# First loads, first 1/std, first transpositions and the v ring of a linear-attention and feed-forward kernel

## The chip, the cores and the metric

The kernel runs on one core of a Trainium2 chip. The metric is the device time of one execution in microseconds (us), lower is better. Every kernel is executed several times, beside the kernel before on the same chip, and one execution is profiled. "Faster" and "slower" are used for differences above 2%.

Engines in the profile: PE is TensorE (matrix products), PEld its weight loads, DVE is VectorE, ACT is ScalarE, POOL is GpSimd, SP is the engine that issues most transfers.

## The reference, cut to what matters

```python
x = A_x                                            # 2048 x 640, bf16
h  = x + A(layernorm(x), wqkv, w_phi, wo)          # 32 heads of 20, two softmax feature maps (+ and -)
h2 = h + B(layernorm(h), w_gate, w_up, w_down)     # (gelu(x Wg) * (x Wu)) Wd, 1536 wide
# in A: pk = k @ w_phi per head; phi_k = [softmax(pk), softmax(-pk)]; kv = phi_k^T v; q likewise; o = phi_q kv / den
```

The kernel cuts the 2048 rows into 16 tiles of 128 rows. It folds w_phi into the q and k weights (products `wa`, evicted to `Wk` and `Wq`), so that k and q tiles come out of one product each.

## The kernel before: the parts that the change and the argument touch

LayerNorm of one tile: statistics on VectorE, 1/std as a power on GpSimd, then the normalised tile on VectorE (`ln`), five 128x128 transpositions on TensorE (`tp`) and a copy to `LN1T`. From tile 6 on, the transposition is done by a DMA.

```python
def ln_stats(pool, tiles, tag, act=True, between=None):
    ...
    ve = small(pool, [P, n], "ve" + tag)
    nc.gpsimd.tensor_scalar_add(ve, mv[:, :, 1], EPS)
    rstd = small(pool, [P, n], "rstd" + tag)
    nc.gpsimd.tensor_tensor(rstd, ve, nhalf[:, 0:n], op=ALU.pow)
```

The first loads come from two issuing engines, and the head of the program is:

```python
nc.sync.dma_start(x_sb[0][:, 0:1, :], x_v[:, 0:1, :])        # tile 0
nc.scalar.dma_start(x_sb[0][:, 1:2, :], x_v[:, 1:2, :])      # tile 1
... # tiles 2-3, Wv, wphi, tiles 4-7, WkT (a DMA transposition)
warm(NWARM)                      # 10 products of zeros, 512 wide
...
ln_st(0, act=False)
ln_st(1, act=False)
ln_ap(0, on_pe=True)
ln_tp(0)
warm(WA)
ln_st(2, act=False, between=lambda: ln_ap(1, on_pe=True))
ln_tp(1)
warm(WB)
ln_st(3, act=False)
ln_ap(2, on_pe=True)
... # BD, the block-diagonal form of w_phi, on VectorE
ln_ap(3, on_pe=True)
v_part(0, 0, 1, 2, 3, 4)
v_part(1, 0, 1)
ln_tp(2)
v_part(1, 2, 3, 4)
ln_tp(3)
v_ev(0)                          # ScalarE evicts v tiles from PSUM to vS
v_ev(1)
v_tile(2)
... # tiles 4 to 7, fold of Wk: evictions in turn by ScalarE (d even) and VectorE (d odd)
```

Then a loop over the 16 tiles: a k tile, its exponentials (`E`), the v tile four ahead, normalisation six ahead, sums and products for the k side (`sk`, `rs`, `vt`), two kv tiles at a time. `vS` is a ring of six v tiles; at tile `T3 = 3` the PSUM pool is exchanged for one with a buffer less, which makes room for `kvp`. The attention of the later tiles is woven into the feed-forward stage:

```python
weave(gus(0, 256, 512) + downs(0, (2, 3)), attn_at(7, 1, SHORT2))   # tile 7 starts at unit 1
```

The softmax here doesn't subtract the row's maximum and nothing guards it: scores larger than these inputs give would overflow.

## Time and profile before

| | before |
|---|---|
| time, median | 281.47 us (280.92 to 281.91, 3 runs); later, beside the changed kernel, 281.43 |
| span of the profiled execution | 279.4 us |
| TensorE busy | 97% |
| first transposition | 6.60 us |
| ScalarE's copy of tile 3's transposition starts | 12.17 us |
| transposition after the first k tile starts | 18.26 us |
| first q product | 62.36 us |
| first 512-wide gate product | 144.07 us |
| last product | 276.15 us |

The timeline from 12 to 19 us, ScalarE and the k tile (start, duration, engine, line, operation, out<-in; the bracket is the idle time before it and what ended it):

```profile
12.17 0.69 ACT L139 COPY LN1T<-tp 128x640 bf16<-128x640 bf16 x1 [1.00 <-PE tp L138]
12.76 1.89 ACT L271 CAST vS<-pv 128x640 bf16<-128x640 f32 x3
14.52 0.72 ACT L224 CAST Wk<-wa 128x640 bf16<-128x640 f32 x1
...
16.11 1.29 ACT L224 CAST Wk<-wa 128x640 bf16<-128x640 f32 x2
16.86 1.57 PE L251 MATMUL pk<-Wk,LN1T 128*128 128x320 bf16 x10 [0.15 <-ACT Wk L224]
```

The copy of the fourth transposition opens a row of eight ScalarE items (itself, three v evictions, a Wk copy, a v eviction, two Wk copies); the k tile begins when the second of its three Wk copies is done. The list of transfers (last number: microseconds from issue to landing), tiles 1 and 0 of x:

```profile
x_sb<-in_A_x_dram ACTq DMA_DIRECT2D x1, 160.0 KB, 3.3
x_sb<-in_A_x_dram SPq DMA_DIRECT2D x1, 160.0 KB, 3.1
```

### The profile page before, as it was taken

Reading aid. Unit: us, or ns where it says so; the run is one execution under the profiler, and the core shown is the slowest. Engines: PE = TensorE matmul, PEld = TensorE weight load, DVE = VectorE, ACT = ScalarE, POOL = GpSimd, SP = SyncE. Lnnn points to the kernel's source line nnn. Section 1 sums busy time; section 2 is a strip of 40 time slices with the busy share of each in tenths; the row PEclk is TensorE's granted clock in tenths of the full one; section 3 lists DMA queues with packets and bytes.
Section 4 is the critical chain, followed back from the end, with each engine's and each line's share of the span. In section 5 each row is a group of like instructions: output and inputs, shape, how many; then the busy total and the mean of one; then the engine's idle time right before and its main releaser. Section 6 shows DMA issues by size and latency. Waiting matters only on the chain.

```text
span 279.4 us, 5750 instructions
## 1 busy us (share of the span) xinstructions
PE 271.9 (97%) x2326; PEld 171.5 (61%) x2326; DVE 166.0 (59%) x289; ACT 139.9 (50%) x226; POOL 96.5 (35%) x211
## 2 busy tenths in 40 slices
PE   5899999999999999999999999999999999999995
PEld 2676677774655788788764555675455567444573
DVE  5899998789396586676324848322667532333222
ACT  2589888758596847355434454413446340222200
POOL 5448986794302216453401243300135230000000
PEclk9999999999999999999999999999999999999999
DMA  7991323694440021322520103221031513000011
GB/s 231 265 260 25 55 49 46 176 396 158 142 145 0 2 45 29 70 50 68 52 70 2 36 20 66 42 77 47 2 47 23 74 23 94 26 1 0 0 49 47
DMA packets 40347, 21.05 MB, mean 75 GB/s; under 512 B 33152, under 2 KB 38400, under 8 KB 40320
## 3 DMA queue, kind: packets, MB, share of 16 engines
q1 hardware_dynamic: 39376, 20.16, 28.8%
q10 hardware_dynamic: 944, 0.52, 0.7%
q8 instruction: 18, 0.29, 0.5%
q14 instruction: 9, 0.07, 0.1%
HBM read 10.18 MB, written 2.62 MB: 46 GB/s over the span
## 4 chain that ended last, share of the span: by engine, by line
PE 89%; DVE 4%; ACT 3%; DMA 1%; POOL 1%; issue 1%; ACTq 0%
PE gu L554 37%; PE pd L569 19%; PE pq L338 8%; PE po L509 8%; PE pk L251 7%; PE pv L251 5%; PE ab L449 2%; PE kvp L316 2%; DVE stats L106 1%; DMA x_sb<-in_A_x_dram 1%; DVE sk L290 1%; ACT E L283 1%; POOL rstd L114 1%; ACT Eq L343 1%; PE wa L215 1%
## 5 line engine op out<-in xcount | busy, mean ns | idle before, releaser
L557 ACT ACTIVATE g<-gu 128x512 bf16<-128x512 f32 (+1 forms) x60 | 30.7, 512 | 76.1 <-PE gu L554 75.1
L560 DVE TENSOR_TENSOR GT<-gu,g 128x512 bf16<-128x512 f32 (+1 forms) x60 | 34.5, 581 | 53.6 <-ACT g L557 53.4
L554 PE MATMUL gu<-LN2T,Wg 128*128 128x512 bf16 (+1 forms) x300 | 61.9, 337 | 0.5 <-DVE GT L560 0.4
L554 PE MATMUL gu<-LN2T,Wu 128*128 128x512 bf16 (+1 forms) x300 | 61.7, 336 | 0.0
L569 PE MATMUL pd<-Wd,GT 128*128 128x320 bf16 x384 | 53.8, 299 | 0.0
L569 PEld LDWEIGHTS <-GT 128*128 128x128 bf16 x384 | 37.4, 98 | 15.7 <-DVE GT L560 0.9
L554 PEld LDWEIGHTS <-Wu 128*128 128x128 bf16 x300 | 29.4, 98 | 22.6
L554 PEld LDWEIGHTS <-Wg 128*128 128x128 bf16 x300 | 28.4, 98 | 21.3 <-issue 0.5
L251 PEld LDWEIGHTS <-LN1T 128*128 128x128 bf16 x300 | 28.5, 98 | 11.6 <-issue 0.7
L298 POOL TENSOR_TENSOR vt<-vS,rs 128x672 bf16<-128x672 bf16 x22 | 29.2, 1345 | 9.1 <-DVE rs L294 8.5
L575 DVE TENSOR_TENSOR y<-pd,x_sb 128x640 bf16<-128x640 f32 (+1 forms) x17 | 13.3, 784 | 30.6 <-PE pd L569 30.6
L457 ACT COPY AB<-ab 128x704 f32<-128x704 f32 x28 | 19.5, 748 | 13.7 <-PE ab L449 13.5
L290 DVE TENSOR_REDUCE sk<-E 128x64 f32<-128x1280 bf16 x16 | 23.3, 1455 | 3.4 <-ACT E L283 3.4
L490 DVE TENSOR_TENSOR tt<-AB,w 128x1280 bf16<-128x1280 f32 x16 | 23.8, 1486 | 2.1 <-POOL w L483 2.0
L251 PE MATMUL pk<-Wk,LN1T 128*128 128x320 bf16 x160 | 24.1, 299 | 0.4 <-ACT E L283 0.3
L509 PE MATMUL po<-Wo,oT 128*128 128x320 bf16 x160 | 24.4, 299 | 0.0
L283 ACT ACTIVATE E<-pk 128x640 bf16<-128x640 f32 x32 | 20.8, 705 | 6.9 <-PE pk L251 6.7
L338 PE MATMUL pq<-LN1T,Wq 128*128 128x512 bf16 x100 | 22.9, 379 | 0.0
L251 PE MATMUL pv<-Wv,LN1T 128*128 128x320 bf16 x140 | 21.3, 299 | 0.0
L343 ACT ACTIVATE Eq<-pq 128x1024 bf16<-128x1024 f32 (+1 forms) x22 | 19.4, 950 | 3.7 <-PE pq L338 3.7
L509 PEld LDWEIGHTS <-oT 128*128 128x128 bf16 x160 | 15.6, 98 | 7.2 <-ACT oT L139 0.2
L125 ACT ACTIVATE ln<-x_sb,v,rstd 128x640 bf16<-128x640 bf16 x14 | 12.9, 919 | 10.5 <-POOL v L537 10.3
(80 smaller groups left out, 258.8 us busy)
## 6 DMA issues: line engine op xcount, KB each, us to landing
out_dram<-y SPq DMA_DIRECT2D x15, 160.0 KB, 1.8
Wg<-in_B_w_gate_dram SPq DMA_DIRECT2D x1, 1920.0 KB, 7.6
Wu<-in_B_w_up_dram SPq DMA_DIRECT2D x1, 1920.0 KB, 15.1
Wd<-in_B_w_down_dram SPq DMA_DIRECT2D x1, 1920.0 KB, 8.0
x_sb<-in_A_x_dram SPq DMA_DIRECT2D x2, 640.0 KB, 4.7
Wo<-in_A_wo_dram SPq DMA_DIRECT2D x1, 800.0 KB, 9.3
x_sb<-in_A_x_dram SPq DMA_DIRECT2D x2, 320.0 KB, 4.8
Wv<-in_A_wqkv_dram SPq DMA_DIRECT2D x2, 320.0 KB, 6.2
```

The lines of the kernel that those rows point to most:

```text
L251: nc.tensor.matmul(ps[:, u, 0:HD], lhsT=lnT(t, c), rhs=W[:, c, u * HD:(u + 1) * HD], start=(c == 0), stop=(c == NC - 1))
L283: nc.scalar.activation(Ek[t][:, s, :].rearrange("p (u f) -> p u f", u=2), pk[:, :, 0:HD], ACTF.Exp, scale=(1.0 if s == 0 else -1.0))
L290: nc.vector.reduce_sum(sk, Ek[t].rearrange("p s (h f) -> p (s h) f", f=Dh), axis=AX.X)
L298: eng.tensor_tensor(vt[:, s], vS[t % 6], rs[:, s * H:(s + 1) * H, None].to_broadcast([P, H, VC]), ALU.mult)
L338: nc.tensor.matmul(pqs[j][:, i, :], lhsT=Wq2[:, kc, c * P:(c + 1) * P], rhs=LN1T[b][:, kc, :], start=(kc == 0), stop=(kc == NC - 1))
L343: nc.scalar.activation(Eq[j][:, :, s, :], pqs[j][:, 0:len(QG[j])], ACTF.Exp, scale=(1.0, -1.0)[s])
L490: nc.vector.tensor_tensor(tt.rearrange("p s (h f) -> p s h f", f=Dh), num, w[:, :, :, None].to_broadcast([P, 2, H, Dh]), ALU.mult)
L509: nc.tensor.matmul(po[:, u, 0:HD], lhsT=st[t][:, c, :], rhs=Wo[:, c, u * HD:(u + 1) * HD], start=(c == 0), stop=(c == NC - 1))
L554: nc.tensor.matmul(gu[:, i, 0:n], lhsT=W[:, c, f * P:(f + 1) * P], rhs=LN2T[b][:, c, a0:a1], start=(c == 0), stop=(c == NC - 1))
L557: nc.scalar.activation(g[:, 0:n], gu[:, 0, 0:n], ACTF.Gelu_apprx_tanh)
L560: nc.vector.tensor_tensor(st[b, "g", f][:, a0:a1], gu[:, 1, 0:n], g[:, 0:n], ALU.mult)
L569: nc.tensor.matmul(pd[:, u, 0:HD], lhsT=st[b, "g", f][:, tl * P:(tl + 1) * P], rhs=Wd[:, f, u * HD:(u + 1) * HD], start=(f == 0), stop=(f ...
```

## The change

The intent, as far as the code tells: bring tile 0 in sooner, shorten the way from its statistics to its normalised form, give TensorE v products as early as they can run, take the ring of v tiles out of VectorE's way, and shorten the last store.

```diff
-    NWARM = 10
+    NWARM = 11
+    KA, QA = (0,1,2,4), (0,1,2,3,4)      # which folds ScalarE evicts (was: even ones)
-    WA, WB = 2,0
-    T3 = 3
+    WA = 1
+    T3 = 4
... ln_stats, for tiles 0, 1 and 2 (log=True)
+            nc.scalar.activation(ve, mv[:, :, 1], ACTF.Ln, bias=eps)
+            nc.scalar.activation(rstd, ve, ACTF.Exp, scale=-0.5)
... ring
-    vS = [... for i in range(6)]
+    vS = [... for i in range(8)]
... loads: all on nc.sync, in the order tile 0, tile 1, Wv 0-3, tiles 2-3, Wv 4, wphi, tiles 4-5, WkT, tiles 6-7
... head
+    ln_st(0, act=False, log=True)
+    ln_st(1, act=False, between=lambda: ln_ap(0, on_pe=True), log=True)
+    ln_tp(0, True)                       # VectorE copies it
     warm(WA)
+    ln_ap(1, on_pe=True)
+    v_part(0, 0, 1)
+    ln_tp(1)
+    ln_st(2, act=False, log=True)
+    v_part(0, 2, 3, 4)
+    v_part(1, 0, 1, 2)
+    ln_st(3, act=False, between=lambda: ln_ap(2, on_pe=True))
+    ln_tp(2)
+    ln_ap(3, on_pe=True)
     ... BD ...
+    v_part(1, 3, 4)
+    v_part(2, 0, 1, 2)
+    ln_tp(3)
+    v_part(2, 3, 4)
     v_ev(0)
     v_ev(1)
+    v_ev(2)
... last tile
+        cuts = [(0, 192), (192, HD)] if last and u == 1 else [(0, HD)]
... weave
-    attn_at(7, 1, SHORT2)
+    attn_at(7, 3, SHORT2)
```

More of the change, by code (lines that the diff above doesn't have):

```diff
@@ L86 @@
     nhalf = const.tile([P, 2], F32, name="nhalf")
+    eps = const.tile([P, 1], F32, name="eps")
     def eq(t, c, s):
@@ L97, in gtile, with ln_stats @@
         return psG.tile([P, 2, 512], F32, name=name, tag="G")
-    def ln_stats(pool, tiles, tag, act=True, between=None):
+    def ln_stats(pool, tiles, tag, act=True, between=None, log=False):
         n = len(tiles)
@@ L111, in ln_stats @@
         ve = small(pool, [P, n], "ve" + tag)
-        nc.gpsimd.tensor_scalar_add(ve, mv[:, :, 1], EPS)
         rstd = small(pool, [P, n], "rstd" + tag)
-        nc.gpsimd.tensor_tensor(rstd, ve, nhalf[:, 0:n], op=ALU.pow)
+        if log:
+            nc.scalar.activation(ve, mv[:, :, 1], ACTF.Ln, bias=eps)
+            nc.scalar.activation(rstd, ve, ACTF.Exp, scale=-0.5)
+        else:
+            nc.gpsimd.tensor_scalar_add(ve, mv[:, :, 1], EPS)
+            nc.gpsimd.tensor_tensor(rstd, ve, nhalf[:, 0:n], op=ALU.pow)
         mr = small(pool, [P, n], "mr" + tag)
@@ L151 @@
     acc = p1.tile([P, NC, 4, VC], F32, name="acc")
-    vS = [p1.tile([P, H, VC], BF16, name=f"vS{i}") for i in range(6)]
+    vS = [p1.tile([P, H, VC], BF16, name=f"vS{i}") for i in range(8)]
     fp_cm = tc.tile_pool(name="fp", bufs=1, side="right", reuse_waits="tile")
@@ L160 @@
     nc.gpsimd.memset(nhalf, -0.5)
+    nc.gpsimd.memset(eps, EPS)
     nc.sync.dma_start(x_sb[0][:, 0:1, :], x_v[:, 0:1, :])
-    nc.scalar.dma_start(x_sb[0][:, 1:2, :], x_v[:, 1:2, :])
+    nc.sync.dma_start(x_sb[0][:, 1:2, :], x_v[:, 1:2, :])
+    nc.scalar.add_instruction(mybir.InstLoadActFuncSet(name=nc.get_next_instruction_name(), act_func_set_id=6))
+    nc.sync.dma_start(Wv[:, 0:2, :], w_v[:, 0:2, 2 * D:3 * D])
+    nc.sync.dma_start(Wv[:, 2:4, :], w_v[:, 2:4, 2 * D:3 * D])
     nc.sync.dma_start(x_sb[0][:, 2:4, :], x_v[:, 2:4, :])
-    for c0, c1 in ((0, 2), (2, 4), (4, 5)):
-        nc.sync.dma_start(Wv[:, c0:c1, :], w_v[:, c0:c1, 2 * D:3 * D])
-    ones = fp.tile([P, 2], F32, name="ones")
-    nc.scalar.activation(ones, nhalf, ACTF.Exp)
-    nc.scalar.dma_start(wphi, phi_v.rearrange("(c p) f -> p c f", p=P))
+    nc.sync.dma_start(Wv[:, 4:5, :], w_v[:, 4:5, 2 * D:3 * D])
+    nc.sync.dma_start(wphi, phi_v.rearrange("(c p) f -> p c f", p=P))
     nc.sync.dma_start(x_sb[1][:, 0:2, :], x_v[:, 4:6, :])
-    nc.scalar.dma_start(x_sb[1][:, 2:4, :], x_v[:, 6:8, :])
     nc.sync.dma_start_transpose(WkT, A_wqkv[:, D:2 * D])
+    nc.sync.dma_start(x_sb[1][:, 2:4, :], x_v[:, 6:8, :])
     wo_v = A_wo.rearrange("(c p) n -> p c n", p=P)
@@ L182 @@
     nc.vector.memset(zero, 0.0)
-    for i in range(6):
+    for i in range(8):
         nc.vector.memset(vS[i][:, :, Dh], 1.0)
@@ L222, in fold @@
                 src = src.rearrange("p u (c f) -> p u c f", c=NC)
-            if d % 2 == 0:
+            if d in (QA if halves else KA):
                 nc.scalar.copy(dst, src)
@@ L228, with ln_st @@
     lnp, Ek, Vt = {}, {}, {}
-    def ln_st(*tiles, act=True, between=None):
-        for t, v in zip(tiles, ln_stats(p1, [x_sb[t // 4][:, t % 4, :] for t in tiles], "1", act, between)):
+    def ln_st(*tiles, act=True, between=None, log=False):
+        for t, v in zip(tiles, ln_stats(p1, [x_sb[t // 4][:, t % 4, :] for t in tiles], "1", act, between, log)):
             lnp[t] = v
@@ L270, in v_ev @@
     def v_ev(t):
-        nc.scalar.copy(vS[t % 6][:, :, 0:Dh].rearrange("p (u h) f -> p u h f", u=2),
+        nc.scalar.copy(vS[t % 8][:, :, 0:Dh].rearrange("p (u h) f -> p u h f", u=2),
                        pv[t][:, :, 0:HD].rearrange("p u (h f) -> p u h f", f=Dh))
@@ L297, in mult @@
         def mult(s, eng):
-            eng.tensor_tensor(vt[:, s], vS[t % 6], rs[:, s * H:(s + 1) * H, None].to_broadcast([P, H, VC]), ALU.mult)
+            eng.tensor_tensor(vt[:, s], vS[t % 8], rs[:, s * H:(s + 1) * H, None].to_broadcast([P, H, VC]), ALU.mult)
         mult(1, nc.gpsimd)
@@ L343, in q_exp @@
             nc.scalar.activation(Eq[j][:, :, s, :], pqs[j][:, 0:len(QG[j])], ACTF.Exp, scale=(1.0, -1.0)[s])
-    ln_st(0, act=False)
-    ln_st(1, act=False)
-    ln_ap(0, on_pe=True)
-    ln_tp(0)
+    ln_st(0, act=False, log=True)
+    ln_st(1, act=False, between=lambda: ln_ap(0, on_pe=True), log=True)
+    ln_tp(0, True)
     warm(WA)
-    ln_st(2, act=False, between=lambda: ln_ap(1, on_pe=True))
+    ln_ap(1, on_pe=True)
+    v_part(0, 0, 1)
     ln_tp(1)
-    warm(WB)
-    ln_st(3, act=False)
-    ln_ap(2, on_pe=True)
+    ln_st(2, act=False, log=True)
[4 more added lines that the diff above has]
+    ln_ap(3, on_pe=True)
     nc.vector.tensor_tensor(BD, wphi[:, :, None, :].to_broadcast([P, NC, 8, Dh]),
                             hmask[:, :, :, None].to_broadcast([P, NC, 8, Dh]), ALU.mult)
-    ln_ap(3, on_pe=True)
-    v_part(0, 0, 1, 2, 3, 4)
-    v_part(1, 0, 1)
-    ln_tp(2)
-    v_part(1, 2, 3, 4)
+    v_part(1, 3, 4)
+    v_part(2, 0, 1, 2)
     ln_tp(3)
+    v_part(2, 3, 4)
     v_ev(0)
     v_ev(1)
-    v_tile(2)
+    v_ev(2)
     ln_st(4, 5, act=False)
@@ L567, in down @@
             pd = gtile("pd")
-        for f in range(NF):
-            nc.tensor.matmul(pd[:, u, 0:HD], lhsT=st[b, "g", f][:, tl * P:(tl + 1) * P],
-                             rhs=Wd[:, f, u * HD:(u + 1) * HD],
-                             start=(f == 0), stop=(f == NF - 1))
         last = b == NB - 1 and tl == 3
-        if u == 1 or last:
-            a = u if last else 0
-            nc.vector.tensor_tensor(y.rearrange("p (u f) -> p u f", u=2)[:, a:u + 1], pd[:, a:u + 1, 0:HD],
-                                    x_sb[b][:, tl, :].rearrange("p (u f) -> p u f", u=2)[:, a:u + 1], ALU.add)
-            stores.append((lag, o_v[:, 4 * b + tl, a * HD:(u + 1) * HD], y[:, a * HD:(u + 1) * HD]))
-            if b == NB - 1 and tl >= 2:
-                store(lag)
+        cuts = [(0, 192), (192, HD)] if last and u == 1 else [(0, HD)]
+        for n0, n1 in cuts:
+            if n0:
+                pd = gtile("pd")
+            for f in range(NF):
+                nc.tensor.matmul(pd[:, u, n0:n1], lhsT=st[b, "g", f][:, tl * P:(tl + 1) * P],
+                                 rhs=Wd[:, f, u * HD + n0:u * HD + n1], start=(f == 0), stop=(f == NF - 1))
+            if u == 1 or last:
+                a = u if last else 0
+                r = lambda x: x.rearrange("p (u f) -> p u f", u=2)[:, a:u + 1, n0:n1]
+                nc.vector.tensor_tensor(r(y), pd[:, a:u + 1, n0:n1], r(x_sb[b][:, tl, :]), ALU.add)
+                f0, f1 = a * HD + n0, u * HD + n1
+                stores.append((lag, o_v[:, 4 * b + tl, f0:f1], y[:, f0:f1]))
+                if b == NB - 1 and tl >= 2:
+                    store(lag)
     later, stores, lag = [], [], 3
@@ L658 @@
           attn_at(6, 13, SHORT2))
-    weave(gus(0, 256, 512) + downs(0, (2, 3)), attn_at(7, 1, SHORT2))
+    weave(gus(0, 256, 512) + downs(0, (2, 3)), attn_at(7, 3, SHORT2))
     for b in range(1, NB):
```

## The prediction

> **What bounds the kernel now.** I read the page first: the busy shares, the slices and the shares of the chain.
>
> ```profile
> PE 271.9 (97%) x2326; PEld 171.5 (61%) x2326; DVE 166.0 (59%) x289; ACT 139.9 (50%) x226; POOL 96.5 (35%) x211
> ...
> PE   5899999999999999999999999999999999999995
> ...
> PE 89%; DVE 4%; ACT 3%; DMA 1%; POOL 1%; issue 1%; ACTq 0%
> ```
>
> TensorE sets the time. Its slices are full except for the first two or three and the last, so only the head, the tail and single waits between can be won. The chain of waits in order of time says when TensorE begins to lead (start, duration, what):
>
> ```profile
> 0.79 3.14 DMA x_sb<-in_A_x_dram
> 3.96 0.90 DVE stats L106 x2
> 4.88 0.21 DVE mv L110
> ...
> 6.67 0.57 POOL rstd L114
> 7.26 0.45 DVE ln L130
> ...
> 9.74 1.42 POOL rstd L114
> 11.18 0.46 DVE ln L130
> 11.63 0.05 issue
> 11.68 0.45 PE tp L138 x5
> 12.13 2.04 PE pv L251 x15
> ...
> 16.21 0.60 ACT Wk L224
> 16.81 0.04 issue
> 16.86 1.57 PE pk L251 x10
> 18.43 0.28 PE tp L138 x5
> ```
>
> Until 11.68 the chain is load, statistics, 1/std and normalised tile, on VectorE and GpSimd. From about 18.4 TensorE's own work leads. From the first transposition at 6.60 to the transposition that follows the first k tile (18.26 in the timeline) TensorE has 5 transpositions of 0.28, 2 warm-up products of 0.22, 40 v products and 10 k products of 0.136 (1.36 for ten) and 5 folds of 0.32: 1.40 + 0.43 + 5.44 + 1.36 + 1.60 = 10.2 us in 11.7, so about 1.4 us of waiting. Later I find one notable wait before the Gelu stage, in the timeline (last bracket: idle before, and its releaser):
>
> ```profile
> 28.86 0.69 ACT L271 CAST vS<-pv 128x640 bf16<-128x640 f32 x1 [0.55 <-DVE vt L298]
> 31.61 0.57 PE L251 MATMUL pk<-Wk,LN1T 128*128 128x320 bf16 x3 [0.28 <-ACT E L283]
> ```
>
> ScalarE waited 0.55 for VectorE to free a v tile, its exponentials came late, and TensorE lost 0.28 here, 0.44 by the starts of its products.
>
> **What the Trainium skill says.** "ScalarE: Activation LUTs", section "What ACT_TABLE_LOAD costs": an activation costs 186 ns + 0.833 ns per element, and some 93 ns more per pointer operand. The trace agrees: 705 ns for E (640 elements, immediates), 919 for ln with two pointers. The same page, "Table sets: the hidden batching unit", puts exp and ln into one set; so the one explicit load should do for both, and the order of the changed kernel's instructions has no further load before Gelu. "SBUF — State Buffer", "SBUF: two separate sides": VectorE and GpSimd share a port pair that is locked for a whole instruction. The trace fits: a 1/std takes 0.57 on GpSimd, but 1.42 at 9.74, beside VectorE's two-input BD (9.75 to 10.72). "DMA: Bandwidth & Descriptors", "Issuing engines are not separate DMA queues": issue from a second engine saves only the sequencer's time; here an issue takes some 0.4 us, so one queue should lose little.
>
> **The change part by part.**
>
> 1. *One queue.* The x tiles 0 and 1 come first and alone; v weights go before tiles 2 and 3, and the many small rows of wphi go later. Tile 0 then no longer shares with tile 1: I estimate its landing at 3.65 instead of 3.9 (0 to 0.5 earlier). The v weights, issued at 1.71 and 2.17 as before, have only 320 KB ahead of them and should land by about 6, against 8; the second half of x tile 1 (tiles 6, 7) goes behind the WkT transposition and lands near 13 to 14, when VectorE wants it at about 14.7. All hidden.
>
> 2. *1/std by Ln and Exp.* GpSimd's way from mean/variance (5.09) to ln (6.10) is 1.01. The new one: two handovers of 0.05, Ln 0.28 (186 + 93, skill), Exp 0.20 (the trace has 0.20 for a 128x2 Exp), 0.04 to VectorE: 0.63. So 0.38 is saved for each of tiles 0, 1 and 2. Tile 3 stays on GpSimd, with BD now after it.
>
> 3. *Order of the first tiles.* I add up from the landing L of tile 0. Statistics 0.90 + 0.21, ready at L+1.13; 1/std L+1.76; ln0 to L+2.21; second half of tile 1's statistics and aggregation to L+2.85; in that gap VectorE also copies transposition 0 (0.48), which frees the first v products at L+3.4, that is 7.05 instead of 8.06. 1/std of tile 1 at L+3.48, ln1 to 3.93, statistics of tile 2 to 5.05; its Ln waits for ScalarE's copy of transposition 1 (to 5.16), so ln2 runs 5.73 to 6.18; the rest of tile 3's statistics to 6.79; GpSimd 1.01; ln3 to 8.25; transposition 0.45; so ScalarE's copy of tile 3 starts at L+8.8 = 12.45. In the kernel before it starts at 12.17. TensorE's work is earlier, the fourth transposition is not, since VectorE got a copy and waits more often.
>
> 4. *From there ScalarE leads.* Before: copy, three vS, Wk, a wait, vS, two Wk, which end at 17.40; TensorE's k tile ends six products later (0.82 + 0.05), at 18.27. After: one more Wk copy stands on ScalarE (four instead of three), no wait: eight spacings of 0.60 and a last 0.70 = 5.5; 12.45 + 5.5 + 0.87 = 18.8. **The head is later by about 0.5**, with an error of 0.6 either way, although the v products begin 1 us earlier.
>
> 5. *Ring of eight, the four-buffer pool for one more tile (T3), all Wq copies on ScalarE.* The wait at 28.86 goes, and with it 0.44 at 31.61: **-0.4**. For tiles 4 to 8 ScalarE then has two E 1.25, vS 0.60, ln 0.85, Wq 0.60 = 3.3 us per tile, TensorE 1.36 + 1.36 + 0.32 + 0.45 = 3.5. Close, but no new bound. VectorE loses 1.5 us of casts.
>
> 6. *The last store in parts of 192 and 128 columns.* The last addition has 128 columns instead of 320: 0.49 becomes about 0.29 (0.82 at 640, 0.49 at 320, in a line); **-0.2**, a little less for the extra product starts.
>
> 7. *Tile 7's attention two units later (offset 3 for 1), which the title does not tell.* Its po products now stand after a last gate/up pair and twelve pd products: 1.09 + 1.64 = 2.73 later. What hangs on them:
>
> ```profile
> 139.75 0.92 ACT L125 ACTIVATE ln<-x_sb,v,rstd 128x640 bf16<-128x640 bf16 x1 [1.49 <-POOL v L537]
> ...
> 140.69 1.20 SPq L141 DMA_TRANSPOSE LN2T<-ln  x1
> ...
> 143.58 0.56 PE L449 MATMUL ab<-KV,Eq 64*128 64x88 bf16 x20
> ...
> 144.07 1.25 PE L554 MATMUL gu<-LN2T,Wg 128*128 128x512 bf16 x5
> ```
>
> This transposition lands 2.6 after its issue (the DMA view's median), at 143.3, and the first 512-wide gate product at 144.07 needs all four tiles: 0.8 to spare. Moved by 2.73, less 0.5 because the square no longer waits behind a Gelu, it lands at 145.5: a **new wait of 1.5 us** just where TensorE had none. Nothing later has slack to give it back.
>
> Sum: +0.5 - 0.4 - 0.2 + 1.5 = +1.4, that is 282.9.
>
> **The rivals.** *The head wins.* If the fourth transposition is not what counts, TensorE can win nearly all its 1.4 us of waits, the 0.4 of part 2 and the 0.25 of part 1: some 2 us, with parts 5 and 6 about 2.6; with part 7 280.4, without it 278.9. For it: v products 1 us earlier, and a tuned order that someone chose. Against it: in program order the evictions of v tiles 0 to 2 stand behind the copy of transposition 3 on ScalarE, so early v products only wait in PSUM. *VectorE keeps up the late start.* It is busy 4.97 of 5 us from 15 to 20, and 9.79 of 10 from 30 to 40; its sums for tile 0 begin at 20.59 and I get about 0.7 later. If the ring does not absorb this, the wait at 31.61 stays: 283.4. *The late tile is hidden.* If the transposition lands faster, or the chain after po is shorter than the one before, part 7 costs 0.5 or nothing: 281.5 to 282.
>
> **Range and chances.** The sum is 282.9. The kernel is tuned and the change presumably meant to gain, so I give the first rival some 40% and place the number at 282.3, with 280.2 to 283.6 eight times in ten. Nothing can win the 5.6 us of 2%: all waits together are smaller. Nor does a loss of 5.6 follow from any part. Faster 1%, within 98%, slower 1%.
>
> **What would show it.** Right: v products start near 7.0; ScalarE's copy of transposition 3 starts at 12.2 to 12.8 and its Wk copies follow without a gap; the tenth k product ends at 18.5 to 19.2; no wait for vS near 28; TensorE idle for 1 to 2 us before the first 512-wide gate product, released by the LN2T transposition. Wrong: a k tile that ends before 18 (parts 3 and 4), or a gate stage that begins without a wait (part 7); then the time is 281 or less.

## The result, and the profile after

The changed kernel took 283.42 us (median of 4 runs, 283.09 to 283.64), the kernel before 281.43 (280.92 to 281.91) beside it. The ratio is 1.0070 [1.0049, 1.0091]. Executions over 1.5% slower than the fastest of the same kernel are left out of the means. Ratios here are the mean time of one kernel's fast runs over that of the other's of the same rounds, so not quite the ratio of the medians; the brackets are 95% intervals. The profiled spans are 281.6 and 279.4 us, both at full granted clock.

The page of the changed kernel, the same three rows as the prediction shows of before:

```profile
PE 274.3 (97%) x2338; PEld 172.4 (61%) x2338; DVE 164.3 (58%) x290; ACT 141.8 (50%) x233; POOL 94.4 (34%) x206
...
PE   8999999999999999999989999999999999999996
...
PE 90%; DMA 3%; ACT 3%; DVE 1%; issue 1%; POOL 0%; POOLq 0%
```

The first two slices of TensorE rose from 5 and 8 to 8 and 9, so TensorE is busier in the head, and one slice in the middle fell to 8: that is the new wait before the gate products. VectorE fell from 4% to 1% of the chain. None of these rows says that the kernel is slower; a busier TensorE is not an earlier one. The times at fixed points say it:

| point | before | after | later by |
|---|---|---|---|
| statistics of tile 0 start | 3.96 | 3.06 | -0.90 |
| first transposition | 6.60 | 5.91 | -0.69 |
| first v product | 8.06 | 7.24 | -0.82 |
| ScalarE's copy of transposition 3 | 12.17 | 12.60 | +0.43 |
| transposition after the first k tile | 18.26 | 18.97 | +0.71 |
| first q product | 62.36 | 63.25 | +0.89 |
| first 512-wide gate product | 144.07 | 146.44 | +2.37 |
| last product | 276.15 | 278.63 | +2.48 |
| end of the span | 279.4 | 281.6 | +2.2 |

The head loses 0.71 in this pair of traces, the tile loop 0.19 more, the wait before the gate stage 1.47; the twelve additional products of the last tile cost 0.11, and after the last product 0.30 are won back (2.99 in place of 3.28), together -0.18. One line of the transfers and one of the timeline give the first row of the table; the tiles now land 2.3 us after their issue, where they took 3.1 and 3.3. (In two experiments below that keep the old loads, shift_alone and ring_alone, the statistics start at 3.70 and 3.86, so the gain is 0.6 to 0.9 from trace to trace.)

```profile
x_sb<-in_A_x_dram SPq DMA_DIRECT2D x2, 160.0 KB, 2.3
...
3.06 0.89 DVE L108 BATCH_NORM_STATS2 stats<-x_sb 128x6 f32<-128x320 bf16 x2 [0.74 <-DMA x_sb<-in_A_x_dram]
```

What became of the 0.9 us is in the chain of waits of the changed kernel (start, duration, what):

```profile
1.24 4.87 PE wu L205 x11
6.12 0.55 PE tp L145 x5
...
7.24 0.72 PE pv L275 x4
7.95 0.28 PE tp L145 x5
8.23 1.77 PE pv L275 x12
10.01 0.39 PE tp L145 x5
...
10.42 0.70 ACT LN1T L146
...
11.16 0.99 PE pv L275 x6
12.15 0.43 PE tp L145 x5
...
12.60 0.70 ACT LN1T L146
```

In the kernel before this chain was load, VectorE and GpSimd until 11.68. Now it is TensorE from the start. Eleven warm-up products take 0.43 each, twice the 0.22 that a 512-wide product takes later (both by the starts; see the caution below); they hold TensorE until 5.91, although the normalised tile 0 is ready at 5.31:

```profile
4.29 0.30 ACT L117 ACTIVATE ve<-mv,eps 128x1 f32<-128x1 f32 x1 [2.22 <-DVE mv L112]
4.62 0.20 ACT L118 ACTIVATE rstd<-ve 128x1 f32<-128x1 f32 x1
4.86 0.45 DVE L137 TENSOR_SCALAR ln<-x_sb,mv,rstd 128x640 bf16<-128x640 bf16 x1 [0.31 <-ACT rstd L118]
```

VectorE's copy of this transposition stands ahead of the normalisation of tile 1 in VectorE's own order, so the delay passes on to that too. Of the later transpositions only the second waits for the v products that were set ahead of it: tile 1 is normalised at 7.53, the fourth of these products hands over at 7.79. Before the third and the fourth the v products and VectorE's normalised tile end almost together, and the timeline puts the start of their weight loads, and with it their own, down to VectorE (tile 2 normalised at 9.87, transposition at 9.93; tile 3 at 12.06, transposition at 12.11):

```profile
12.11 0.28 PEld L145 LDWEIGHTS <-ln 128*128 128x128 bf16 x5 [0.29 <-DVE ln L137]
```

From the copy of the fourth on, ScalarE works without a gap through nine items, four of them Wk copies, until 18.07:

```profile
12.60 0.69 ACT L146 COPY LN1T<-tp 128x640 bf16<-128x640 bf16 x1 [1.50 <-PE tp L145]
13.19 1.89 ACT L279 CAST vS<-pv 128x640 bf16<-128x640 f32 x3
14.94 1.33 ACT L232 CAST Wk<-wa 128x640 bf16<-128x640 f32 x2
16.11 0.76 ACT L279 CAST vS<-pv 128x640 bf16<-128x640 f32 x1
16.70 1.37 ACT L232 CAST Wk<-wa 128x640 bf16<-128x640 f32 x2
17.61 1.52 PE L259 MATMUL pk<-Wk,LN1T 128*128 128x320 bf16 x10 [0.25 <-DVE Wk L234]
```

The k tile ends at 18.97, 0.90 after the last Wk copy. In the loop the wait for a vS buffer is gone, but TensorE now waits for transpositions of LN1T by DMA, which are issued when ScalarE has normalised a tile; from the chain of waits:

```profile
25.06 2.56 DMA LN1T<-ln
...
27.67 1.55 PE pv L259 x10
```

By the starts of the products TensorE loses 0.27 at 27.26, 0.29 at 33.68 and 0.19 at 45.06, against 0.08 at 26.56 and 0.44 at 31.03 before. The wait near 27 did not come from ScalarE: this transposition is issued 6.09 us after the end of the k tile in the changed kernel (25.06 after 18.97) and 6.10 in the kernel before (24.36 after 18.26). It takes longer: 2.56 from issue to landing where the kernel before has 2.37, and these 0.19 are the difference of the two waits. Last, the timeline before the gate stage:

```profile
142.88 0.92 ACT L132 ACTIVATE ln<-x_sb,v,rstd 128x640 bf16<-128x640 bf16 x1 [1.49 <-POOL v L546]
...
144.49 0.57 PE L458 MATMUL ab<-KV,Eq 64*128 64x88 bf16 x20
...
146.44 1.25 PE L563 MATMUL gu<-LN2T,Wg 128*128 128x512 bf16 x5 [1.38 <-DMA LN2T<-ln]
```

The normalised tile 7 is ready at 143.8, its transposition lands at 146.4, and TensorE has been out of work since its twenty small products at 144.49.

**A caution on the clock.** TensorE begins at half speed (512-wide products 0.43 apart) and reaches full speed (0.22 apart) at some point that differs from run to run. By the starts of its products in the profiled executions that is 4.0 us in the kernel before, between 6.4 and 7.2 in the changed one, and 5.0 to 10.2 in the experiments with ten or eleven warm-up products. So single traces differ by some 0.5 us in the head for no reason of the program: undo_shift below has the head of the changed kernel, and ends its first k tile at 18.44 in place of 18.97. The times of one kernel also fall into two groups (before: 280.7 to 281.2 and 281.6 to 281.8 in the first set below); whether that is the clock too is not shown. The head is therefore judged by the ratios of many runs, and by pairs of traces with the same moment of full speed.

### The profile page after: what moved, and what is told of

It is laid out like the page before. It is cut to its first block, busy times and chain, and to the rows that moved or that the text cites. A ratio compares the mean times of both kernels' runs of the same rounds, so it can differ in the third digit from the quotient of the medians.

```text
span 281.6 us, 5785 instructions
## 1 busy us (share of the span) xinstructions
PE 274.3 (97%) x2338; PEld 172.4 (61%) x2338; DVE 164.3 (58%) x290; ACT 141.8 (50%) x233; POOL 94.4 (34%) x206
## 4 chain that ended last, share of the span: by engine, by line
PE 90%; DMA 3%; ACT 3%; DVE 1%; issue 1%; POOL 0%; POOLq 0%
PE gu L563 37%; PE pd L584 17%; PE pq L346 8%; PE po L518 8%; PE pk L259 6%; PE pv L259 6%; PE kvp L324 2%; PE ab L458 2%; DMA LN1T<-ln 2%; PE wu L205 2%; PE pv L275 1%; ACT ln L132 1%; PE tp L145 1%; DMA LN2T<-ln 1%; PE wa L223 1%
## 5 line engine op out<-in xcount | busy, mean ns | idle before, releaser
L584 PE MATMUL pd<-Wd,GT 128*128 128x320 bf16 (+2 forms) x396 | 54.0, 295 | 0.0
L584 PEld LDWEIGHTS <-GT 128*128 128x128 bf16 x396 | 38.0, 98 | 15.4 <-DVE GT L569 0.9
L259 PEld LDWEIGHTS <-LN1T 128*128 128x128 bf16 x290 | 27.4, 98 | 12.1 <-DMA LN1T<-ln 1.0
L306 POOL TENSOR_TENSOR vt<-vS,rs 128x672 bf16<-128x672 bf16 x22 | 29.8, 1372 | 9.8 <-DVE rs L302 8.1
L589 DVE TENSOR_TENSOR y<-pd,x_sb 128x640 bf16<-128x640 f32 (+3 forms) x18 | 13.5, 750 | 28.6 <-PE pd L584 28.6
L259 PE MATMUL pv<-Wv,LN1T 128*128 128x320 bf16 x130 | 20.0, 299 | 0.5 <-ACT LN1T L146 0.2
L132 ACT ACTIVATE ln<-x_sb,v,rstd 128x640 bf16<-128x640 bf16 x14 | 12.9, 920 | 12.4 <-POOL v L546 12.2
```

Source lines behind the costliest of these rows:

```text
L259: nc.tensor.matmul(ps[:, u, 0:HD], lhsT=lnT(t, c), rhs=W[:, c, u * HD:(u + 1) * HD], start=(c == 0), stop=(c == NC - 1))
L306: eng.tensor_tensor(vt[:, s], vS[t % 8], rs[:, s * H:(s + 1) * H, None].to_broadcast([P, H, VC]), ALU.mult)
L584: nc.tensor.matmul(pd[:, u, n0:n1], lhsT=st[b, "g", f][:, tl * P:(tl + 1) * P], rhs=Wd[:, f, u * HD + n0:u * HD + n1], start=(f == 0), sto ...
```

## The experiments

Theory after the result: the loss has three sources, the attention of tile 7 two units later (+1.5), a head led by ScalarE and by the order on TensorE (+0.7), and a ring that gains nothing. Main rival: the head does gain, and something in the loop or the whole of the loss is elsewhere. Each experiment ran in 6 executions beside 11 of the kernel before (the changed kernel itself in 4 beside 4). The times:

| kernel | median us | before beside it | ratio to before |
|---|---|---|---|
| changed kernel | 283.42 | 281.43 | 1.0070 [1.0049, 1.0091] |
| undo_shift | 281.69 | 281.10 | 1.0022 [1.0007, 1.0036] |
| shift_alone | 282.56 | 281.10 | 1.0053 [1.0037, 1.0068] |
| ring_alone | 281.53 | 281.10 | 1.0024 [1.0006, 1.0043] |
| warm8 | 285.36 | 281.10 | 1.0138 [1.0116, 1.0160] |
| u_vev | 281.38 | 281.65 | 0.9988 [0.9973, 1.0003] |
| u_t3 | 281.72 | 281.65 | 1.0000 [0.9984, 1.0015] |
| queue_alone | 280.82 | 281.65 | 0.9965 [0.9948, 0.9982] |
| queue_log | 280.94 | 281.65 | 0.9968 [0.9945, 0.9990] |
| u_nolog | 282.12 | 281.63 | 1.0020 [0.9997, 1.0043] |
| u_vev_ln | 281.28 | 281.63 | 0.9989 [0.9968, 1.0010] |
| q_best | 281.12 | 281.63 | 0.9986 [0.9963, 1.0008] |
| queue_tail | 280.43 | 281.46 | 0.9962 [0.9941, 0.9983] |

All gave correct results.

### undo_shift: the changed kernel with tile 7 where it was

```diff
-    attn_at(7, 3, SHORT2)
+    attn_at(7, 1, SHORT2)
```

> The changed kernel with tile 7's attention put back by two units (offset 1), all else kept. Theory: the whole 1.5 us wait before the first 512-wide gate product is due to this move; it vanishes (below 0.1) and the time falls from 283.4 by 1.4 to 1.6, to about 281.9. Rival (the transposition comes late for another reason, such as the later start of everything before it): a wait of 1 us or more stays and the time stays above 282.8.

The ratio fell from 1.0070 to 1.0022, some 1.35 us. Its timeline before the gate stage shows no wait:

```profile
144.31 0.57 PE L458 MATMUL ab<-KV,Eq 64*128 64x88 bf16 x20
...
144.80 1.25 PE L563 MATMUL gu<-LN2T,Wg 128*128 128x512 bf16 x5
```

About two thirds of the loss is this one number. The rest, 1.0022 or 0.6 us, is left to head, loop and tail together. A pair of traces splits it: in undo_shift and in shift_alone, the next experiment, which has the head and loop of the kernel before, every product from the first transposition on runs at full speed. The first k tile ends at 18.44 and 17.99, the first q product starts at 63.07 and 62.02. So, in one trace each, the new head costs 0.45 and the new loop 0.60 (it waits 0.28 at 26.73 and 0.84 at 33.16 for LN1T, shift_alone 0.43 once), and the tail gives 0.2 back. With the warm-up products done at 5.44, the chain of waits in this head starts from the x tiles 2 and 3, which the change loads behind most of the v weights:

```profile
2.70 4.46 DMA x_sb<-in_A_x_dram
```

### shift_alone: the kernel before with tile 7 moved

```diff
-    attn_at(7, 1, SHORT2)
+    attn_at(7, 3, SHORT2)
```

> The kernel before with tile 7's attention two units later (offset 3) and nothing else. Theory: the same wait appears, 1.4 to 1.6 us before the first 512-wide gate product, and the time rises by as much, to about 282.9. Rival (it needs the late head to hurt): at most 0.5 us.

1.5 us slower than the kernel before, and the wait appears at the same place and from the same releaser, in a kernel with none of the other parts:

```profile
143.24 0.57 PE L449 MATMUL ab<-KV,Eq 64*128 64x88 bf16 x20
...
145.18 1.25 PE L554 MATMUL gu<-LN2T,Wg 128*128 128x512 bf16 x5 [1.37 <-DMA LN2T<-ln]
```

Done alone and undone alone, the move is worth the same within 0.15 us by the ratios (their intervals are wider than that). The wait is there without the new head.

### ring_alone: the kernel before with ring of eight, T3 = 4 and all Wq copies on ScalarE

```diff
-    T3 = 3
+    T3 = 4
-    vS = [... for i in range(6)]          # and t % 6 -> t % 8
+    vS = [... for i in range(8)]
-            if d % 2 == 0:
+            if d in ((0, 1, 2, 3, 4) if halves else (0, 2, 4)):
```

> The kernel before with the ring of eight v tiles, the four-buffer pool for one more tile and all Wq casts on ScalarE, nothing else. Theory of the prediction: ScalarE's wait of 0.55 for a v tile near 28.9 goes, TensorE's 0.44 at 31.6 with it, time lower by 0.3 to 0.5. Rival, from the changed kernel's trace, where TensorE waits 0.27 and 0.29 for DMA transpositions of LN1T near 27 and 34 instead: the wait only changes its cause, time within 0.15 of before.

No gain: 1.0024, in two groups (four runs near 281.5, two near 282.5). The trace:

```profile
29.13 0.69 ACT L271 CAST vS<-pv 128x640 bf16<-128x640 f32 x1 [0.30 <-PE pv L251]
...
29.87 1.52 PE L251 MATMUL pk<-Wk,LN1T 128*128 128x320 bf16 x10 [0.78 <-ACT vS L271]
```

The wait of 0.55 for VectorE in front of a vS copy is gone, as meant. But TensorE waits 0.27 for a transposition of LN1T (at 27.15, by the starts), and 0.95 at 28.79 for a k tile that needs the PSUM buffer of the v tile just copied: it is the first tile after the exchange of the pool. (This trace is of one of the two slow runs, with full speed only at 10.2; whether the four others wait here is not known.) Before, the two waits in this stretch came to 0.5. So the ring took one wait away and two others took its place; the -0.4 falls. The transposition near 27 takes 2.56 here too, in a kernel with the old head. All the traces say the same: from 23 to 28 us LN1T's transpositions take 2.36 to 2.39 in the five kernels with six v tiles and GpSimd's 1/std throughout, and 2.55 to 2.58 in the nine with a ring of eight or with Ln and Exp, both of which change the tiles held in SBUF. Why is not shown; where the tiles lie in memory is a guess that no run tests. Nor does a run separate the ring from the Wq copies.

### warm8: the changed kernel with eight warm-up products

```diff
-    NWARM = 11
+    NWARM = 8
```

> The changed kernel with 8 warm-up products instead of 11. In its trace the eleven ran at half clock (0.427 each) until 5.91, while the first normalised tile was ready at 5.31. Theory (the warm-up products hold up the first transposition): it starts at about 5.4, and the first k tile 0.3 to 0.5 earlier, time about 283.0. Rival (fewer products leave the array at half clock for longer, and that eats it): the v products after it run at 0.267 each for some us, no gain or a loss of up to 0.5.

This asked whether the warm-up products that hold TensorE until 5.91 are the cost. Taking three away made it 1.9 us slower than the changed kernel (runs from 283.76 to 285.65):

```profile
1.24 3.59 PE L205 MATMUL wu<-zero 128*128 128x512 bf16 x8 [1.24 <-DVE zero L190]
5.37 0.71 PE L145 MATMUL tp<-ident,ln 128*128 128x128 bf16 x5 [0.53 <-DVE ln L137]
...
8.24 2.98 PE L275 MATMUL pv<-Wv,LN1T 128*128 128x320 bf16 x12
```

The transposition starts 0.54 sooner, as the theory had it. But the twelve v products that took 1.94 in the changed kernel take 2.98 here: TensorE stayed at half speed until 10.6 us. The k tile ends 0.94 later than in the changed kernel and the first q product starts 1.27 later; another 0.9 of this run is a wait at 208.5 for a transposition of oT, far from the head, so not all of the 1.9 is shown to be the clock. My guess that the warm-ups were simply too many was wrong. Nor is it shown that the gap of half a microsecond after them is what kept the speed at half: of two kernels with ten warm-ups and a gap of 0.6 to 0.8 us behind them, ring_alone ran at half speed until 10.2, and shift_alone was at full speed by 6.33.

### u_vev: undo_shift with the v evictions of tiles 0 and 1 ahead of the copy of transposition 3

```diff
     v_part(1, 3, 4)
+    v_ev(0)
+    v_ev(1)
     v_part(2, 0, 1, 2)
     ln_tp(3)
     v_part(2, 3, 4)
-    v_ev(0)
-    v_ev(1)
     v_ev(2)
```

> The changed kernel with tile 7 put back, and the evictions of v tiles 0 and 1 set before the copy of transposition 3 on ScalarE. Theory of the prediction (from that copy on ScalarE leads the head): the last Wk copy ends about 0.5 earlier than the 18.07 of the changed kernel's trace, and the first k tile starts 0.4 to 0.6 earlier than 17.61; time 281.2 against 281.7. Rival (VectorE's Wk copy, which ends at 17.56 behind two normalisations that wait for GpSimd, releases the first k tile): ScalarE is earlier, the k tile is not, time the same within 0.15.

0.9988 against undo_shift's 1.0022. The trace can be set beside that of the changed kernel, since both reach full speed between 6.4 and 7.2 and are alike up to 10.4:

```profile
11.01 1.30 ACT L279 CAST vS<-pv 128x640 bf16<-128x640 f32 x2
...
12.59 0.69 ACT L146 COPY LN1T<-tp 128x640 bf16<-128x640 bf16 x1 [0.29 <-PE tp L145]
...
14.54 1.29 ACT L232 CAST Wk<-wa 128x640 bf16<-128x640 f32 x2 [0.66 <-PE wa L223]
...
16.30 1.32 ACT L232 CAST Wk<-wa 128x640 bf16<-128x640 f32 x2
```

Two of the nine items fit into ScalarE's idle time before the copy, which itself starts at the same 12.59. The last Wk copy ends at 17.62 instead of 18.07, the k tile starts at 17.07 instead of 17.61 and ends 0.42 sooner. It is not the whole 1.2 of two items: ScalarE now waits 0.66 for the fold, and inside the k tile one product waits 0.12 for VectorE's own Wk copy. This shows that ScalarE led in the changed kernel, and by how little it led.

### u_t3: undo_shift with the pool exchanged one tile earlier, as before

```diff
-    T3 = 4
+    T3 = 3
```

> The changed kernel with tile 7 put back, and the PSUM pool exchanged at k tile 3 as in the kernel before instead of 4. Theory (from the run of the ring parts alone, where the k tile at the exchange waited 0.95 for the eviction of a v tile): the exchange at 4 costs time, so this is 0.3 or more faster, about 281.3. Rival (in the changed kernel's own trace that k tile has no wait): the same within 0.15, or slower where the fourth buffer is missed.

1.0000 against 1.0022, in different sets; the intervals overlap, so at most 0.2% and not shown. The waits for LN1T (0.28 and 0.52 by the starts) are there as in undo_shift (0.28 and 0.84), so the exchange of the pool is not what makes them. What T3 alone is worth stays open.

### queue_alone: the kernel before with all first loads on one queue, in their old order of use

```diff
-    nc.scalar.dma_start(x_sb[0][:, 1:2, :], x_v[:, 1:2, :])
+    nc.sync.dma_start(x_sb[0][:, 1:2, :], x_v[:, 1:2, :])
-    nc.scalar.dma_start(wphi, ...)
+    nc.sync.dma_start(wphi, ...)
-    nc.scalar.dma_start(x_sb[1][:, 2:4, :], x_v[:, 6:8, :])
+    nc.sync.dma_start(x_sb[1][:, 2:4, :], x_v[:, 6:8, :])
```

> The kernel before with all first loads on one queue, in the old order of use (x tiles 0 to 3, v weights, wphi, x tiles 4 to 7, then the transposition of Wk). Theory: tile 0 lands near 3.1 instead of 3.9, as in the changed kernel's trace, the old chain behind it is as long as before, so the first k tile starts 0.6 to 0.9 earlier (about 16.1) and the time falls by as much, to about 280.3. Rival (something else becomes late, such as the v weights or the transposition of Wk, or the clock of the array, which is independent of the loads): less than 0.3 is won.

0.9965: of the parts that were tried alone, the one that pays by itself. Its six runs (280.40 to 281.08) lie below all eleven of the kernel before (281.19 to 282.38). The timeline:

```profile
3.04 0.89 DVE L106 BATCH_NORM_STATS2 stats<-x_sb 128x6 f32<-128x320 bf16 x2 [1.00 <-DMA x_sb<-in_A_x_dram]
...
11.22 0.69 ACT L139 COPY LN1T<-tp 128x640 bf16<-128x640 bf16 x1 [0.79 <-PE tp L138]
...
13.55 0.80 PE L216 MATMUL wa<-BD,WkT 128*128 128x140 bf16 x12 [0.34 <-DMA WkT<-in_A_wqkv_dram]
```

With the load as early as in the changed kernel (3.04) but the old order, the copy of transposition 3 starts at 11.22. In the changed kernel it starts at 12.60. **The new head costs 1.4 us on exactly the item that opens ScalarE's row** (0.9 against undo_shift, where it starts at 12.08 with the warm-ups ending at 5.44), and that is where the 0.9 us of the sooner load went. Not all of it is the order of work: x tiles 2 and 3 land at 5.65 here and at 7.13 in the changed kernel, and there are ten warm-ups here in place of eleven. No run separates these. Here the k tile ends at 17.82, held by WkT, which in the one queue is issued at 5.19 instead of 4.52 and lands at 13.5. The trace of before (18.26) is 0.44 later; it fell in a run with early full speed (4.0 against 7.1), which may be why the times show more.

### queue_log: queue_alone with 1/std of tiles 0 to 2 by Ln and Exp

```diff
... a tile eps, and the explicit table load in place of a first Exp
-    ln_st(0, act=False)
-    ln_st(1, act=False)
+    ln_st(0, act=False, log=True)
+    ln_st(1, act=False, log=True)
...
-    ln_st(2, act=False, between=lambda: ln_ap(1, on_pe=True))
+    ln_st(2, act=False, between=lambda: ln_ap(1, on_pe=True), log=True)
```

> The same with 1/std of tiles 0, 1 and 2 by Ln and Exp on ScalarE, in the old order of work. Theory: 0.3 more than the run with the queue alone, about 280.0; ln of tile 0 starts as soon as tile 1's statistics allow. Rival: in the old order tile 0's normalisation stands behind tile 1's statistics on VectorE, which end when GpSimd's 1/std is ready too, so Ln and Exp win nothing for tile 0 and at most 0.1 in all.

0.9968 beside 0.9965: nothing won. VectorE is done with tile 1 sooner, but then waits for x tile 2, which lands at 6.48 (at 5.65 in queue_alone, with the same loads, so this pair of traces is a poor test), and the copy of transposition 3 comes at 11.65, later than queue_alone's 11.22. The k tiles start alike (16.38 and 16.41), since queue_alone loses its lead waiting for WkT, and queue_log then has a wait of 1.02 at 24.73 in the loop (by the starts).

### u_nolog: undo_shift with all 1/std on GpSimd

```diff
-    ln_st(0, act=False, log=True)
-    ln_st(1, act=False, between=lambda: ln_ap(0, on_pe=True), log=True)
+    ln_st(0, act=False, log=False)
+    ln_st(1, act=False, between=lambda: ln_ap(0, on_pe=True), log=False)
...
-    ln_st(2, act=False, log=True)
+    ln_st(2, act=False, log=False)
```

> The changed kernel with tile 7 put back and 1/std of tiles 0, 1 and 2 on GpSimd again, in the new order of work. Theory: in the new order these steps are on the chain; tile 0's 0.38 hides behind the warm-up products, tiles 1 and 2 lose 0.3 to 0.4 each, so ScalarE's copy of transposition 3 and the first k tile come 0.5 to 0.8 later, time 282.3 against 281.7. Rival (Ln and Exp win as little here as they did in the old order): within 0.2.

1.0020 against undo_shift's 1.0022: no difference that the intervals can tell, less than I expected. The chain of waits says why for tile 0:

```profile
4.65 0.58 POOL rstd L121
5.25 0.45 DVE ln L137
```

The normalised tile 0 starts at 5.25 instead of 4.86, yet the first transposition starts at 5.91 in both: the warm-up products are the later of the two. The normalised tile 3 starts 0.28 later (11.89, in the changed kernel 11.61), and the k tile 0.19 later (17.80 for 17.61).

### u_vev_ln: u_vev with the normalisation ahead of the v eviction in the loop

```diff
-            v_tile(t + 4)
+            v_mm(t + 4)
         if t > 0 and t + 6 < NT:
             ln_ap(t + 6, on_act=True)
+        if t + 4 < NT:
+            v_ev(t + 4)
```

> The changed kernel with tile 7 put back, early evictions of v tiles 0 and 1, and in the loop over k tiles the normalisation of tile t+6 before the eviction of v tile t+4 on ScalarE. Theory (the waits near 27 and 33 are a loop: v product, its eviction, normalisation, DMA transposition, v product; ScalarE's order makes it 0.6 too long): both waits, 0.27 and 0.39, go, time 0.4 to 0.6 lower than the 281.4 of the run without this. Rival (the transposition waits for its place on the queue or for its landing, whatever ScalarE does): the waits stay, same time within 0.15.

0.9989, the same as u_vev. The waits moved: the one near 27 (0.27) is gone, the next grew from 0.39 to 0.55, and one of 0.19 came at 40.35; 0.74 in place of 0.66, all by the starts of the products. The second wait did not yield to ScalarE's order at all: the transposition that it waits for was issued 1.3 us sooner than in u_vev (29.06 for 30.35), but took 4.24 instead of 3.31 and landed at 33.30 for 33.66:

```profile
29.06 4.24 DMA LN1T<-ln
```

That is the rival of the expectation (the landing, whatever ScalarE does). In the kernel before the same transposition takes 2.90; what makes it slow stays open.

Its head ended 0.25 sooner than u_vev's (full speed at 5.0 instead of 6.4 to 7.2), and 0.18 of that were left at the first q product.

### q_best: queue_alone, WkT ahead of tiles 6 and 7, the eviction of v tile 0 early, eleven warm-ups, the tail of the change

```diff
-    NWARM = 10
+    NWARM = 11
     ... WkT issued before x tiles 6-7, ln_st(6) moved next to ln_st(7)
     v_part(1, 2, 3, 4)
+    v_ev(0)
     ln_tp(3)
-    v_ev(0)
     v_ev(1)
     ... last store in 192 + 128 columns
```

> An attempt at the best of both: the old order of work with one queue, the transposition of Wk before x tiles 6 and 7, whose statistics move behind the fold of Wk, the eviction of v tile 0 before the copy of transposition 3, eleven warm-up products, and the last store in two parts. Theory: the wait of 0.5 for the transposition of Wk, seen with one queue alone, goes, 0.2 are won at the tail and some tenths by the eviction: about 280.0, that is 1.2 to 1.6 below the kernel before. Rival (the late statistics delay the first exponentials' sums, or the clock of the array decides): not below 280.6.

The head came out best so far: the k tile ends at 17.36, 0.46 before queue_alone's. At the first q product the lead is gone (62.31 against 62.25). In between, TensorE waits 0.63 at 28.87 and 0.59 at 30.79, where queue_alone waits 0.42 and 0.40. The chain of waits runs through VectorE in this stretch:

```profile
20.91 1.36 DVE sk L291
...
26.54 1.35 DVE sk L291
27.89 0.78 DVE vt L299
```

A k tile that starts sooner finds VectorE with its statistics still to do, more so since I had put those of tile 6 later. The gain of the head is only kept as far as VectorE can follow. The ratio, 0.9986, is no better than that of queue_alone.

### queue_tail: queue_alone and the tail of the change

```diff
+        cuts = [(0, 192), (192, HD)] if last and u == 1 else [(0, HD)]
     ... products, addition and store per cut
```

> The kernel before with two parts of the change: all first loads on one queue in their old order of use, and the last output tile finished and stored in parts of 192 and 128 columns. The one queue alone gave 0.9965 of the kernel before [0.9948, 0.9982]. Tail theory (my -0.2): in the trace the last addition takes 0.29 in place of 0.49, twelve more products start, and the stretch from the first 512-wide gate product to the end of the span is 0.15 to 0.25 shorter than the 135.3 of the kernel before; the time is 0.9955 to 0.996 of it, 280.4 to 280.7. Rival: the second half of the store or the extra products take it back, the stretch is 135.3 again and the ratio 0.9965 or more. The ratio itself may not tell 0.2 us apart; the stretch in the trace can.

0.9962 and 280.43 us, the fastest kernel. The stretch from the first 512-wide gate product to the end is 278.58 - 143.42 = 135.16 us, against 279.32 - 143.95 = 135.37 in queue_alone and 279.43 - 144.07 = 135.36 in the kernel before: the tail is worth 0.2, as in the changed kernel (135.18). It cannot be told from the ratio.

## Why the prediction was right or wrong, point by point

The time fell into the predicted range, near its upper end: 283.42 for a range up to 283.6 and a number of 282.3. The hand sum, 282.9, was closer than the number that I drew from it.

1. *One queue.* Right in direction, mis-sized: tile 0 was to land 0.25 earlier and its statistics began 0.9 earlier. "One queue should lose little" was too small a thought: alone it won 0.35%. I read the rule on issuing engines as "no difference", where sharing meant that the transfer wanted first landed nearly as late as the one wanted second (3.94 and 4.12 in the kernel before).
2. *Ln and Exp.* The 0.63 from statistics to normalised tile measured 0.67 (4.19 to 4.86; the terms as written add up to 0.62). But the step held that 0.38 is saved for tile 0, and the warm-up products hid that; undone (u_nolog) and added to the queue (queue_log) the saving in time is within the noise.
3. *Order.* The structure was right, the copy of transposition 3 is not sooner but later. Counted from the landing it came at 9.5 (12.60 - 3.06) instead of 8.8. What I left out is that TensorE itself would be in the chain: the warm-ups at half speed hold the first transposition 0.6 behind its tile, and with it VectorE's copy and the next normalisation; in undo_shift, where they end 0.5 sooner, the copy comes at 9.0 (12.08 - 3.04). The v products ahead of a transposition add at most 0.3, once. The new place of x tiles 2 and 3 in the queue would hold a faster head: in undo_shift, u_t3, u_vev_ln and warm8 the statistics of tile 2 start 0.02 to 0.03 after its landing at 7.0 to 7.4. The landing of tile 0, 0.6 sooner than estimated, hid this error, so that 12.60 lies inside the 12.2 to 12.8 by two errors that cancel.
4. *ScalarE leads.* Right: 5.47 for the row (5.5 predicted), k tile's end 0.90 after it (0.87), at 18.97 (18.8). u_vev confirms the cause. It led by little in the changed kernel: VectorE's Wk copy ended at 17.56, and it is what the k tile's start is put down to.
5. *Ring, pool and Wq copies.* **This is the step that failed.** It was to give -0.4; the stretch gave +0.2, and ring_alone shows no gain without the other parts. The wait for vS went, as predicted; the step then assumed that TensorE's 0.44 went with it. In its place came waits for LN1T's DMA transposition (0.27 and 0.29) and, with ring_alone, for a PSUM buffer (0.95). That each engine's work per tile fits into TensorE's 3.5 us was true and did not help: the sum had no term for the transposition's time from issue to landing, which went from 2.37 to 2.56 for the first and from 2.90 to 3.21 for the second. What lengthens it stays open.
6. *Tail.* -0.2 predicted, -0.18 in the changed kernel, -0.21 in queue_tail. Right.
7. *Tile 7 two units later.* +1.5 predicted; +1.47 in the trace, +1.5 alone, -1.35 undone. The transposition was to land at 145.5; with the head's 0.9 that is the 146.4 that was measured. Right, and two thirds of the loss.

Of the rivals, "the head wins" did not come: v products did start sooner, and waited. Giving it 40% is what drew the number down to 282.3. "VectorE keeps up the late start" had the right time, 283.4, by another way: the waits that came were for the landing of LN1T, not for VectorE. "The late tile is hidden" is refuted by shift_alone.

What stays open: whether the split of undo_shift's remainder into head (0.45) and loop (0.60), from one pair of traces, holds over many runs; why LN1T's transpositions take longer; what T3 = 4 alone is worth; and why the times of queue_alone show 1.0 us where its trace shows 0.1 at the first q product (the profiled run of before was of the quick group, 281.18).

## What to carry to other kernels

A change of many parts is to be priced part by part, and the smallest line of the diff, here a 1 that became a 3, can weigh more than the rest; whatever moves a producer later is to be followed to its consumer, with the transfer's time added. What stands ahead of a critical item in an engine's program order (warm-ups before a transposition, evictions before or after a copy) counted for more in this head than how fast each step is: two evictions moved were worth 0.42 at the k tile, Ln and Exp 0.19. When a wait is removed, look which wait ends next in the same stretch before counting the gain, and whether a transfer still takes as long as it did.

## What the Trainium skill lacked or had wrong

- "TensorE: Matmul & The Clock Gate", section "Part 1: The HAM clock gate (the "warmup" mystery)": it says that whatever is issued in the first 3.4 us or so runs at half clock and everything after at full clock, with a window that runs freely, and that the cost is below 1% of a span. That the point varies agrees: full speed at 4.0 to 10.2 us in the runs with ten or eleven warm-up products, the first of which starts at 1.24. The 3.4 us do not bound it: half speed lasted 9.0 us in ring_alone, with a pause of 0.8 in it. What it lacks is what a short pause does: half speed until 10.6 with eight products (1.24 to 4.83) and half a microsecond without work, until 10.2 with ten and a longer pause, but full speed by 6.33 with ten and a pause of 0.6. The kernel with eight was 1.9 us or 0.7% slower than with eleven, part of it far from the head; against effects of 0.2% that is not small.
- "DMA: Bandwidth & Descriptors", section "Issuing engines are not separate DMA queues": right that a second issuing engine adds no engines and that the transfers interleave, but the only effect that it names is the sequencer's time that is saved. It lacks what interleaving costs the one wanted first: two loads of 160 KB issued at 0.79 from two engines took 3.1 and 3.3 us, issued one after the other from one engine 2.3 each, and the first user began 0.6 to 0.9 us earlier.
- "ScalarE: Activation LUTs", section "What ACT_TABLE_LOAD costs": agrees (Ln with a pointer bias on 128x1 took 0.30, Exp with immediates 0.20, a table load 1.28). I found no page with a duration for the handover from one engine to the next, which is a quarter of this path: 0.67 from the end of the statistics to the start of the normalised tile, of which the two activations are 0.50.
- No page that I found says that one and the same DMA transposition takes longer in one kernel than in another: LN1T's took 2.37 us in the kernel before and 2.56 in the changed one, with the same form.
